# Last input block of an expert's up-projection as two full-height products, with every engine's order written anew

## The chip, the cores and the metric

The program runs on one core of a Trainium2 chip. A core has five engines that run at the same time, each on its own list of instructions, and that wait for each other through semaphores: TensorE (PE; its weight loads are shown apart as PEld), VectorE (DVE), ScalarE (ACT), GpSimd (POOL) and SyncE (SP), which here issues most of the DMA transfers. Products are accumulated in eight banks of PSUM, each 128 partitions by 512 float32 columns. The metric is the device time of one execution in microseconds (us); lower is better.

## The reference

An mLSTM-like recurrence is followed by two gated experts, all in float32:

```python
for t in range(S):                                   # S = 768, B = 2, H = 8, D = 40
    m_new = np.maximum(f_gate[:, :, t] + m, i_gate[:, :, t])
    ...
    C = f_stab[:, :, None, None] * C + i_stab[:, :, None, None] * np.einsum('bhd,bhe->bhde', vt, kt)
    n = f_stab[:, :, None] * n + i_stab[:, :, None] * kt
    h_tilde = np.einsum('bhde,bhe->bhd', C, qt)
    denom = np.maximum(np.abs(np.einsum('bhd,bhd->bh', n, qt)[:, :, None]), 1.0)
    y[:, :, t] = sigmoid(o_gate[:, :, t]) * h_tilde / denom
...
x = y.transpose(0, 2, 1, 3).reshape(1536, 320)
xn = x / rms(x) * rms_g                              # first expert
x = (silu(xn @ w_gate) * (xn @ w_val)) @ w_out       # 320 -> 1536 -> 320
x = (sigmoid(x @ w_gate2) * (x @ w_val2)) @ w_out2   # second expert, same sizes
```

## The kernel before

**The recurrence** is done in blocks of 128 steps: 6 blocks for each of 2 batches, so 12 units u of 128 tokens. For a unit, TensorE makes the decay exponents (`A`, line 425 for the first block of a batch, lines 432 and 435 later, from rows `rows3` that are sent there by DMA), the scores q·k (`S`, line 459, 40 rows high), the outputs (`O`, lines 483 and 492) and the update of the state (`C`, lines 519 and 521). The gates' running sums and maxima (`g1` to `g9`) are made once at the start on VectorE from the loaded gates `fi`; the running maximum goes to DRAM and back (`gO`, `gI`, tile `mD`) to be laid out for the later blocks, and then as `rows3` to the units from u = 2 on.

**The experts.** Each has 12 blocks m of 128 hidden columns, and tokens go in 3 groups g of 512, so there are 2 x 3 x 12 = 72 up-projections. To keep float32 accuracy with the fast fp32r format, each operand is split into a rounded part (hi) and the rest (lo), and three products are summed: hi·hi, lo·hi and hi·lo. The 320 input channels are two blocks of 128 and a last one of 64. In `xT` the last block stands twice, in partitions 0 to 63 and 64 to 127 (column blocks 2 for hi and 5 for lo). In the weights of that block, hi stands in one half of the partitions and lo in the other (`w_lo` writes the lo half). So one full product of x block 2 gives hi·hi and lo·hi together; only hi·lo is left over, from x block 5 and the hi half of the weights.

`up` (lines 622 to 634) makes the gate (`ug`, j = 0) and the value (`uv`, j = 1) of one block, each into one bank with the tag `wk`, of which there are four. In each, seven full products come from line 631: six for the first two blocks, and one for block 2. With the gate, line 634 makes the two leftover products of half height, the gate's from one half of the partitions and the value's from the other. Then ScalarE takes tanh (`ht`, line 638), VectorE multiplies (`hg`, `hv`), ScalarE rounds (`hh`), VectorE takes the rest (`hl`), and four `dn` of three products each (lines 662 to 664) add the block to the 320 outputs. `fn` and `st` take the outputs away.

**Weights** come as float64 in 48 halves of 544 KB (`wl`, SP queue), and ScalarE and VectorE turn each into hi and lo (`wp`, `wq`, `wb`, `wh`, `ws`).

**The order.** `ORDER` is a list of some 1,590 step names. The program is written by walking this list, so it fixes the order of each engine's instructions, those of the SP queue too. An engine takes its list in order, and what stands behind a waiting instruction waits too; only TensorE's weight loads (PEld) run beside the product ahead of them. Steps named `k` are products of zeros (line 391) into a bank that isn't used yet; they compute nothing and keep TensorE at work.

Of the kernel before, what the change touches and what calls it, by code (L numbers as in the profile page):

```python
# [44 lines left out]
HALF = (slice(0, 64), slice(64, 128))  # L45
# [11 lines left out]
Nd2 wq1 C2 Sb3 wp5 Sa3 Ab5 Ma3 Ws3 Lb3 Eg3 Lc3 U2 Ab4 Mb3 Xb4 Ga3 Gb3 P3 wh2 Oa3 Ob3 Ne2 wl0 k18 Nf2 wq5 ws2 wb5 Na3
Nb3 Lb4 Ld4 Xb5 k6 Wv3 cw4 La4 Nc3 Sa4 cw1 Sb4 Wp4 Ws4 Nd3 Dc3 C3 Ga4 Eg4 P4 wb1 wh1 U3 wl4 Mb4 Gb4 Lc4 wh5 wq4 wp4
Aa5 Oa4 Ob4 La5 Ld5 Ne3 ws1 Sb5 Na4 Nf3 ws5 wq0 Nb4 Ng2 Nc4 Aa6 Lb5 Dc4 Sa5 Wp5 Ws5 Wv4 C4 Xa5 Ma5 Lc5 P5 k45 Ga5 Ng3
Oa5 Nd4 Ne4 U4 d0.2 Xa6 Mb5 Gb5 wp0 wl9 wl10 Ob5 Na5 Wv5 Ma6 wb0 wh0 Nb5 Wp6 Eg5 Nc5 La6 Sa6 Ga6 Dc5 Aa7 Ab6 Xb6 Sb6  # L60
Ld6 C5 Ws6 wb4 Mb6 Nf4 P6 Lb6 Oa6 Gb6 Ob6 Nd5 Ab7 Ld7 La7 Lc6 U5 Ne5 Nf5 wh4 Xa7 Ma7 Na6 Ng4 ws4 Xb7 Eg6 Lb7 Lc7 Wp7
Ab9 Xb9 Mb7 Wv6 Nb6 Nc6 Nd6 Sa7 Sb7 C6 wl6 d0.4 wq6 Ws7 Gb7 Wv7 d0.1 P7 Aa8 Ga7 Oa7 Ne6 Dc6 wp6 Ob7 U6 wp9 La8 wq10
Ng5 ws0 Wp8 Ld8 Eg7 Na7 Nb7 Nc7 Ws8 Xa8 Sa8 Ab8 Xb8 Ma8 Ga8 Mb8 Sb8 Gb8 La9 C7 Lb8 Dc7 U7 Nd7 Wv8 P8 Eg8 Aa9 Xa9 d0.0
Mb9 Oa8 Lc8 Ld9 Ob8 Na8 Ma9 Sb9 Wp9 Nb8 Nc8 Ws9 Sa9 Ga9 t0.0 wb6 Gb9 Lb9 Eg9 Lc9 C8 P9 d0.3 Oa9 Ob9 Aa11 Dc8 Nf6 wl12
U8 Ng6 t0.1 x0.0 wh6 y0.0 wp10 Na9 Nb9 Nc9 x0.1 y0.1 Xa11 Ab10 Dc9 Xb10 t0.2 Wv9 C9 U9 Ld10 Ab11 La10 Wp10 Ws10 x0.2
Aa10 Xb11 Sa10 y0.2 Xa10 Wp11 Ma10 Ga10 Ma11 P10 t0.3 x0.3 y0.3 Mb10 Ne7 Nf7 Sb10 Gb10 wq9 La11 Sa11 ug0.0.0 Ld11 Ws11
Nd8 Ga11 Ng7 ht0.0.0 wb9 wb10 ws6 wh10 wh9 wp12 wq12 ug0.0.2 wl15 uv0.0.0 ht0.0.2 wq15 ws9 uv0.0.2 hg0.0.0 wb12
hv0.0.0 Nd9 hh0.0.0 ws10 wp15 hl0.0.0 hg0.0.2 hv0.0.2 wh12 Lb10 ws12 wl8 ug0.0.1 P11 wp8 ht0.0.1 hg0.0.1 hh0.0.2
hl0.0.2 wb15 Eg10 wl7 uv0.0.1 hv0.0.1 wq7 Oa10 Ob10 wh15 ws15 d0.5 Lb11 Eg11 Sb11 Ne8 wl16 Na10 wp7 wb7 Mb11 ug0.0.3
Gb11 wp16 hh0.0.1 wq8 ht0.0.3 wb8 wh8 dn0.0.0.0 Oa11 Ne9 Nf9 hg0.0.3 ws8 Nf8 d0.7 wq16 wb16 wl11 wp11 Ob11 wh7 ws7  # L70
Nb10 wh16 ug0.0.4 wq11 wl18 wp18 Nc10 uv0.0.4 Na11 Nb11 Ng8 t0.4 dn0.0.0.2 uv0.0.3 hl0.0.1 ht0.0.4 wl13 wq13 Nc11
# [75 lines left out]
def attention_then_two_moe(tc, fi, fir, qk, qt3, nat, w1, w2, rms_g, consts, out, order):  # L147
    nc = tc.nc
    ctx = ExitStack()
    cp = ctx.enter_context(tc.tile_pool(name="cp", bufs=1))  # L150
# [448 lines left out]
    for u in range(NU):  # L599
# [9 lines left out]
        for hh in range(2):  # L609
            h = "ab"[hh]  # L610
# [11 lines left out]
    def up(moe, g, m, j):  # L622
# [7 lines left out]
        for i, (a, b) in enumerate(terms):  # L630
            nc.tensor.matmul(o, lhsT=a, rhs=b, start=(j == 0 and i == 0), stop=(j == 1 and i == 6))  # L631
# [144 lines left out]
```

## Time and profile before

| | before |
|---|---|
| median of three runs | 532.69 us (530.91 to 535.45) |
| the profiled execution, device time | 533.24 us |
| its span, first to last instruction | 531.5 us |
| TensorE busy | 519.5 us (98%) |
| VectorE, ScalarE, GpSimd busy | 265.2, 213.4, 50.8 us |
| mean granted TensorE clock | 0.965 of full |

The span is 1.7 us less than the device time of the same execution. In the profile a line such as `L631 PE MATMUL wk<-xT,wH` is one group of instructions: the line of the kernel, the engine, the operation, and the tile written from the tiles read. The duration of one product is its passage through the array and overlaps the next one, so a product's cost is read from the distance between starts. A float32 product of the recurrence shows as two records.

### The profile page before, as it was taken

Reading aid. Unit: us, or ns where it says so; the run is one execution under the profiler, and the core shown is the slowest. Engines: PE = TensorE matmul, PEld = TensorE weight load, DVE = VectorE, ACT = ScalarE, POOL = GpSimd, SP = SyncE. Lnnn points to the kernel's source line nnn. Section 1 sums busy time; section 2 is a strip of 40 time slices with the busy share of each in tenths; the row PEclk is TensorE's granted clock in tenths of the full one; section 3 lists DMA queues with packets and bytes.
Section 4 is the critical chain, followed back from the end, with each engine's and each line's share of the span. In section 5 each row is a group of like instructions: output and inputs, shape, how many; then the busy total and the mean of one; then the engine's idle time right before and its main releaser. Section 6 shows DMA issues by size and latency. Waiting matters only on the chain.

```text
span 531.5 us, 7232 instructions
## 1 busy us (share of the span) xinstructions
PE 519.5 (98%) x2801; PEld 424.2 (80%) x2801; DVE 265.2 (50%) x504; ACT 213.4 (40%) x415; POOL 50.8 (10%) x102
## 2 busy tenths in 40 slices
PE   5999999999999999999999999999999999999997
PEld 4788989877887787878887778787887787887876
DVE  3546876497976344434455576745432222232213
ACT  3525553376675222223234568635431222222112
POOL 4024644200100000000000000000000000000000
PEclk9958997698999999999999999999999999999999
DMA  6475855264443010001002345502000000020001
GB/s 169 123 208 158 239 192 183 72 208 143 159 129 93 36 42 1 0 1 42 1 0 86 102 132 187 169 8 77 1 1 25 1 0 1 1 74 1 0 1 50
DMA packets 15252, 41.43 MB, mean 78 GB/s; under 512 B 1874, under 2 KB 6530, under 8 KB 15218
## 3 DMA queue, kind: packets, MB, share of 16 engines
q1 hardware_dynamic: 14882, 40.56, 25.0%
q8 instruction: 22, 0.36, 0.3%
q10 hardware_dynamic: 336, 0.41, 0.2%
q14 instruction: 12, 0.10, 0.1%
HBM read 38.77 MB, written 2.01 MB: 77 GB/s over the span
## 4 chain that ended last, share of the span: by engine, by line
PE 85%; ACT 0%; issue 0%
PE wk L631 46%; PE wk L634 6%; PE dn L662 5%; PE at L662 5%; PE dn L664 4%; PE at L664 4%; PE dn L663 4%; PE at L663 4%; PE at L492 2%; PE wk L583 2%; PE wk L459 2%; PE at L483 1%; PE at L519 1%; PE wk L432 0%; PE wk L435 0%; PE at L470 0%
## 5 line engine op out<-in xcount | busy, mean ns | idle before, releaser
L631 PE MATMUL wk<-xT,wH 128*128 128x512 f32 x720 | 216.8, 402 | 0.0
L631 PEld LDWEIGHTS wk<-xT,wH 128*128 128x128 f32 x720 | 128.5, 188 | 29.0 <-issue 8.1
L642 DVE SCALAR_TENSOR_TENSOR th<-th,wk 128x512 f32<-128x512 f32 x72 | 48.9, 685 | 112.8 <-PE wk L631 71.5
L631 PE MATMUL wk<-xT,wL 128*128 128x512 f32 x288 | 90.8, 397 | 0.0
L638 ACT ACTIVATE th<-wk 128x512 f32<-128x512 f32 x72 | 42.6, 596 | 114.1 <-PE wk L634 109.9
L650 ACT CAST hT<-th 128x512 fp32r<-128x512 f32 x72 | 44.1, 619 | 81.3 <-DVE th L642 29.9
L654 DVE TENSOR_TENSOR hT<-th,hT 128x512 fp32r<-128x512 f32 x72 | 48.9, 689 | 50.2 <-ACT hT L650 49.6
L631 PEld LDWEIGHTS wk<-xT,wL 128*128 128x128 f32 x288 | 54.5, 189 | 12.7
L662 PE MATMUL dn<-wH,hT 128*128 128x320 f32 x144 | 47.5, 330 | 0.0
L662 PE MATMUL at<-wH,hT 128*128 128x320 f32 x144 | 46.6, 324 | 0.0
L664 PE MATMUL dn<-wH,hT 128*128 128x320 f32 x144 | 44.6, 310 | 0.0
L664 PE MATMUL at<-wH,hT 128*128 128x320 f32 x144 | 44.5, 309 | 0.0
L663 PE MATMUL dn<-wL,hT 128*128 128x320 f32 x144 | 44.5, 309 | 0.0
L663 PE MATMUL at<-wL,hT 128*128 128x320 f32 x144 | 44.5, 309 | 0.0
L199 DVE SCALAR_TENSOR_TENSOR wT<-wT,w 128x544 int32<-128x544 int32 x48 | 34.3, 722 | 11.8 <-ACT wT L190 9.6
L190 ACT ACTIVATE wT<-wraw 128x544 f32<-128x544 f32 x48 | 33.0, 695 | 8.5 <-DVE wL L217 3.2
L634 PE MATMUL wk<-xT,wH 64*128 64x512 f32 x144 | 36.4, 500 | 0.0
L634 PEld LDWEIGHTS wk<-xT,wH 64*128 64x128 f32 x144 | 13.5, 184 | 26.9 <-issue 26.9
L206 ACT CAST wH<-wT 128x544 fp32r<-128x544 f32 x48 | 30.2, 641 | 11.0 <-DVE wT L199 8.9
L195 ACT ACTIVATE w<-wraw 128x544 int32<-128x544 uint16 x48 | 33.3, 698 | 1.2 <-DMA wraw<-in_w_dram 1.2
L459 PE MATMUL wk<-qk 40*128 40x128 f32 x192 | 29.4, 316 | 4.4 <-DMA qk<-in_qk_dram 4.4
L662 PEld LDWEIGHTS dn<-wH,hT 128*128 128x128 f32 x144 | 27.2, 189 | 6.6 <-issue 5.3
(114 smaller groups left out, 604.3 us busy)
## 6 DMA issues: line engine op xcount, KB each, us to landing
wraw<-in_w_dram SPq DMA_DIRECT2D x48, 544.0 KB
nat<-in_nat_dram SPq DMA_DIRECT2D x12, 324.0 KB
qk<-in_qk_dram SPq DMA_DIRECT2D x24, 160.0 KB
qt<-in_qt_dram SPq DMA_DIRECT2D x10, 180.0 KB
nat<-in_nat_dram SPq DMA_DIRECT2D x10, 180.0 KB
out_dram<-x2n SPq DMA_DIRECT2D x10, 160.0 KB
out_dram<-x2n ACTq DMA_DIRECT2D x2, 160.0 KB
rows<-x2n SPq DMA_DIRECT2D x6, 30.0 KB
```

Source lines behind the costliest of these rows:

```text
L195: nc.scalar.activation(t, upper, AF.Copy, scale=2.0 ** -13, bias=FLOOR)
L199: nc.vector.scalar_tensor_tensor(out=t, in0=t, scalar=3, in1=w3.pop(k), op0=ALU.logical_shift_left, op1=ALU.bitwise_or)
L459: nc.tensor.matmul(o[:, h * L:(h + 1) * L], lhsT=d["qk"][r, 1, h, :], rhs=d["qk"][r, 0, h, :], start=True, stop=True)
L631: nc.tensor.matmul(o, lhsT=a, rhs=b, start=(j == 0 and i == 0), stop=(j == 1 and i == 6))
L634: nc.tensor.matmul(act[moe, g, m][k], lhsT=hi[h, 128 * k:128 * (k + 1)], rhs=x[h, 5, :], start=(k == 1), stop=(k == 0))
L638: nc.scalar.activation(th, act[moe, g, m][0], AF.Tanh, scale=0.5)
L642: nc.vector.scalar_tensor_tensor(out=th, in0=th, scalar=1.0, in1=act[moe, g, m][moe], op0=ALU.add, op1=ALU.mult)
L650: Copy(hT[:, 0, :], act[moe, g, m, "h"])
L654: TT(out=hT[:, 1, :], in0=th, in1=hT[:, 0, :].bitcast(F32), op=ALU.subtract)
L662: nc.tensor.matmul(o, lhsT=hi, rhs=wo[0], start=(m == 0), stop=False)
L663: nc.tensor.matmul(o, lhsT=hi, rhs=wo[1], start=False, stop=False)
L664: nc.tensor.matmul(o, lhsT=lo, rhs=wo[0], start=False, stop=(m == NM - 1))
```

## The change

In `up`, the leftover product hi·lo of the last block is no longer made from a half-height weight for gate and value side by side. Instead x block 5 (lo, which stands in both halves of the partitions) is multiplied at full height with the same weights as x block 2, hi in one half and lo in the other. Gate and value each have eight full products in place of seven and a share in a pair of half-height ones; the small term lo·lo is now added too. Each bank's sum is opened and closed by its own eight products.

The list `ORDER` is new as a whole; two of its lines stand in the diff below. The steps in it are the same but for the `k` steps, which were 14 and are 11.

```diff
 ORDER = """
-cj cr cm cb ck wl3 gF gS La0 Lb0 g1 Ma0 g3 wp3 wq3 cs ci Sa0 gR Aa0 g2 ga gb ge Xa0 Sb0 wl2 gC Mb0 Ab0 Ga0 Xb0 Gb0 Ld2
+cj ci gS gF k46 ck k40 wl0 k28 gR k21 wl3 k31 cb k56 gC cm k55 cr g1 La0 k20 cs k33 Mb0 Ma0 Ma1 g3 Ab0 wq0 g2 gO k35
...
         terms = [((hi, lo)[r][:, at[r] + 128 * i:at[r] + 128 * (i + 1)], x[:, sl, :]) for r, i, sl in UP_TERMS]
-        terms.append((hi[:, 128 * j:128 * (j + 1)], x[:, 2, :]))
+        terms += [(hi[:, 128 * j:128 * (j + 1)], x[:, sl, :]) for sl in (2, 5)]
         for i, (a, b) in enumerate(terms):
-            nc.tensor.matmul(o, lhsT=a, rhs=b, start=(j == 0 and i == 0), stop=(j == 1 and i == 6))
-        if j == 0:
-            for k, h in enumerate(HALF):
-                nc.tensor.matmul(act[moe, g, m][k], lhsT=hi[h, 128 * k:128 * (k + 1)], rhs=x[h, 5, :], start=(k == 1), stop=(k == 0))
+            nc.tensor.matmul(o, lhsT=a, rhs=b, start=(i == 0), stop=(i == 7))
```

On TensorE, at the gate's up-projection of one block in the experts (`wH` and `wL` are one block's weights, `hT` the hidden values that `dn` takes), before:

```order
L631 MATMUL wk<-xT,wH_1526 128x512 x4
L631 MATMUL wk<-xT,wL_1527 128x512 x2
L631 MATMUL wk<-xT,wH_1526 128x512
L634 MATMUL wk<-xT,wH_1526 128x512 x2
L662 MATMUL at<-wH_1195,hT 128x320
```

and in the changed kernel:

```order
L658 MATMUL at<-wH_1180,hT 128x320
L659 MATMUL at<-wL_1181,hT 128x320
L660 MATMUL at<-wH_1180,hT 128x320
L630 MATMUL wk<-xT,wH_1715 128x512 x4
L630 MATMUL wk<-xT,wL_1716 128x512 x2
L630 MATMUL wk<-xT,wH_1715 128x512 x2
L582 MATMUL wk<-ident,x2n 128x128 x3
L630 MATMUL wk<-xT,wH_1715 128x512 x4
L630 MATMUL wk<-xT,wL_1716 128x512 x2
```

The two half-height rows of line 634 are gone, and the last `wH` row of each side counts two instead of one.

On TensorE at the very start of the program, from its first instruction, before (`masks` are constant tiles, `qk` the loaded queries and keys):

```order
L420 LDWEIGHTS masks
L420 MATMUL wk<-masks 128x512
L459 MATMUL wk<-qk 128x128 x4
L425 MATMUL wk<-x2n,ident 128x128 x4
L287 MATMUL at<-ident,x2n 128x16
L459 MATMUL wk<-qk 128x128 x4
L420 LDWEIGHTS masks
```

and in the changed kernel from the eighth of the zero products on (line 390, tile `junk`); seven like it stand ahead of these:

```order
L390 LDWEIGHTS junk
L390 MATMUL dn<-junk 128x512
L390 LDWEIGHTS junk
L390 MATMUL dn<-junk 128x512
L419 LDWEIGHTS masks
L419 MATMUL wk<-masks 128x512
L419 LDWEIGHTS masks
L419 MATMUL wk<-masks 128x512
L419 LDWEIGHTS masks
L419 MATMUL wk<-masks 128x512
L424 MATMUL wk<-x2n,ident 128x128 x4
L390 LDWEIGHTS junk
```

Nine zero products and three of the mask products now stand ahead of everything else, and the scores, which came second, come after them.

On TensorE ahead of the first product that reads `rows3`, before:

```order
L391 MATMUL dn<-junk 128x512
L391 LDWEIGHTS junk
L391 MATMUL dn<-junk 128x512
L459 MATMUL wk<-qk 128x128 x8
L432 LDWEIGHTS rows_0_75
L432 MATMUL wk<-pick,rows_0_75 128x512
```

and in the changed kernel:

```order
L518 MATMUL at<-wv,nat 120x123 x2
L518 MATMUL at<-wv,nat 120x82
L491 MATMUL at<-nat,E 128x41 x8
L518 MATMUL at<-wv,nat 120x123 x2
L518 MATMUL at<-wv,nat 120x82
L431 LDWEIGHTS rows_0_75
L431 MATMUL wk<-pick,rows_0_75 128x512
```

The second unit's outputs (line 492, now 491) and state update (line 519, now 518), which came later, now stand ahead of that product, and the zero products there are gone.

On the SP queue at the start (`wraw` is a half of the weights, `x2n<-in_fi` the gates of the first block), before:

```order
L186 DMA wraw<-in_w_dram 128x1088
L298 DMA x2n<-in_fi_dram 16x2x128
L407 DMA qk<-in_qk_dram 40x1024 x2
L410 DMA nat<-in_nat_dram 128x648
L300 DMA x2n<-in_fir_dram 80x256
L186 DMA wraw<-in_w_dram 128x1088
L302 DMA cst<-in_consts_dram 80x144
L415 DMA qt<-in_qt_dram 120x384
L306 DMA mD<-x2n 16x641
```

and in the changed kernel:

```order
L297 DMA x2n<-in_fi_dram 16x2x128
L185 DMA wraw<-in_w_dram 128x1088
L299 DMA x2n<-in_fir_dram 80x256
L185 DMA wraw<-in_w_dram 128x1088
L301 DMA cst<-in_consts_dram 80x144
L406 DMA qk<-in_qk_dram 40x1024 x2
L305 DMA mD<-x2n 16x641
L409 DMA nat<-in_nat_dram 128x648 x2
L276 DMA x2n<-mD 80x1x129
```

The gates' load has moved ahead of the first weight half, and the queries and keys behind the second. On POOL the fill of the zero tile and of `reset` (step `cr`), which `g1` reads, has moved from the front to behind the identity, the block pattern and the masks.

## Rows read from the trace of the kernel before

**Rows 1.** The page's first part: busy us (share of span) and instructions of each engine.

```profile
PE 519.5 (98%) x2801; PEld 424.2 (80%) x2801; DVE 265.2 (50%) x504; ACT 213.4 (40%) x415; POOL 50.8 (10%) x102
```

**Rows 2.** Stretches: width, then busy us of PE, PEld, DVE, ACT, POOL; clock, DMA, GB/s.

```profile
0.00:17.50 17.50, 10.99 (x43) 9.26 (x44) 5.41 (x15) 5.14 (x12) 5.46 (x24) 1.00 0.68 189
...
27.80:44.80 17.00, 17.00 (x82) 14.94 (x82) 8.21 (x20) 4.03 (x11) 4.02 (x7) 0.50 0.59 185
44.80:82.40 37.60, 37.23 (x332) 33.43 (x329) 29.50 (x68) 21.08 (x50) 21.62 (x31) 1.00 0.70 210
82.40:85.80 3.40, 3.40 (x18) 3.12 (x18) 2.27 (x4) 0.54 (x3) 2.84 (x5) 0.50 0.06 19
...
89.20:102.90 13.70, 13.70 (x70) 12.58 (x71) 7.62 (x16) 4.06 (x9) 1.59 (x2) 0.50 0.39 133
...
123.40:126.80 3.40, 3.40 (x10) 2.03 (x9) 1.24 (x3) 1.29 (x3) 1.23 (x3) 0.51 0.77 206
126.80:527.80 401.00, 401.00 (x2035) 322.21 (x2033) 185.34 (x326) 155.18 (x281) 7.12 (x19) 1.00 0.16 49
```

**Rows 3.** Groups by line: busy us, mean ns | idle before, what ended it.

```profile
L634 PE MATMUL wk<-xT,wH 64*128 64x512 f32 x144 | 36.4, 500 | 0.0
...
L634 PEld LDWEIGHTS wk<-xT,wH 64*128 64x128 f32 x144 | 13.5, 184 | 26.9 <-issue 26.9
...
L631 PEld LDWEIGHTS wk<-xT,wH 128*128 128x128 f32 x720 | 128.5, 188 | 29.0 <-issue 8.1 <-DVE xT L597 0.5
```

**Rows 4.** Timeline of PE in the steady stage: start, time, instruction.

```profile
399.80 1.09 PE L631 MATMUL wk<-xT,wH 128*128 128x512 f32 x4
...
403.05 0.31 PE L662 MATMUL dn<-wH,hT 128*128 128x320 f32 x1
...
403.94 1.08 PE L631 MATMUL wk<-xT,wH 128*128 128x512 f32 x4
...
405.32 0.40 PE L631 MATMUL wk<-xT,wH 128*128 128x512 f32 x1
405.66 0.50 PE L634 MATMUL wk<-xT,wH 64*128 64x512 f32 x2
406.09 1.20 PE L631 MATMUL wk<-xT,wH 128*128 128x512 f32 x4
407.13 0.62 PE L631 MATMUL wk<-xT,wL 128*128 128x512 f32 x2
...
407.82 0.31 PE L662 MATMUL dn<-wH,hT 128*128 128x320 f32 x1
```

**Rows 5.** Timeline of PE in the first 31 us.

```profile
7.12 2.07 PE L459 MATMUL wk<-qk 40*128 40x128 f32 x8 [4.09 <-DMA qk<-in_qk_dram]
...
22.73 1.71 PE L459 MATMUL wk<-qk 40*128 40x128 f32 x16
25.23 0.38 PE L432 MATMUL wk<-pick,rows 120*128 120x512 bf16 x1 [0.79 <-DMA rows<-x2n]
...
26.10 0.38 PE L391 MATMUL dn<-junk 128*128 128x512 bf16 x1
26.32 0.33 PE L470 MATMUL at<-rows,wide 120*120 120x128 bf16 x3
27.32 3.20 PE L492 MATMUL at<-nat,E 128*128 128x41 f32 x16 [0.66 <-DVE qt L475]
```

**Rows 6.** Timeline of DVE at the start.

```profile
0.89 0.11 DVE L377 MEMSET junk<- 128x64 uint32 x1 [0.89 <-PEq L766]
...
6.42 0.59 DVE L268 TENSOR_TENSOR_SCAN x2n<-x2n 16x128 f32<-16x128 f32 x1 [5.42 <-DMA x2n<-in_fi_dram]
```

**Rows 7.** Timeline of the SP queue: the round trip of the running maxima.

```profile
9.74 0.31 SPq L306 DMA_DIRECT2D mD<-x2n  x1
11.72 0.60 SPq L277 DMA_DIRECT2D x2n<-mD  x1
```

**Rows 8.** Stretch from 100 to 150 us, columns as in rows 2.

```profile
100.00:150.00 50.00, 50.00 (x276) 40.30 (x275) 39.28 (x81) 32.87 (x64) 7.03 (x13) 0.94 0.46 147
```

More of the change, by code (lines that the diff above doesn't have):

```diff
@@ L57 @@
[L57 to L71, printed above, removed]
@@ new lines @@
+uv0.1.1 ht0.1.1 hg0.1.1 dn0.1.0.2 hv0.1.1 dn0.1.0.0 uv0.1.3 hh0.1.1 hl0.1.1 t0.8 dn0.1.0.1 x0.8 dn0.1.0.3 y0.8
+dn0.1.1.3 hv0.1.3 dn0.1.1.0 dn0.1.2.0 hh0.1.3 dn0.1.1.1 wp26 hl0.1.3 dn0.1.2.3 dn0.1.2.1 ug0.1.4 uv0.1.4 ht0.1.4
+hg0.1.4 ug0.1.5 t0.9 dn0.1.3.3 x0.9 dn0.1.3.0 ht0.1.5 dn0.1.3.1 hg0.1.5 uv0.1.5 hv0.1.4 ug0.1.6 hv0.1.5 y0.9 dn0.1.1.2
+dn0.1.2.2 t0.10 hh0.1.4 uv0.1.6 x0.10 hl0.1.4 wq26 y0.10 hh0.1.5 ht0.1.6 dn0.1.4.1 hl0.1.5 ug0.1.7 wp24 hg0.1.6 wb26
+hv0.1.6 uv0.1.7 ht0.1.7 hg0.1.7 dn0.1.5.1 hv0.1.7 dn0.1.3.2 dn0.1.4.2 hh0.1.6 dn0.1.4.3 hl0.1.6 dn0.1.5.3 ug0.1.8
@@ new lines @@
+ug0.2.1 hv0.2.0 dn0.1.11.3 ht0.2.1 dn0.1.11.0 fn0.1.3 hg0.2.1 ug0.2.2 wq32 y1.0 hh0.2.0 fn0.1.0 hl0.2.0 t1.1
+dn0.1.11.2 x1.1 uv0.2.1 ht0.2.2 fn0.1.2 dn0.2.0.1 hv0.2.1 ug0.2.4 y1.1 hh0.2.1 hg0.2.2 hl0.2.1 dn0.1.11.1 ht0.2.4
+uv0.2.2 fn0.1.1 d1.5 d1.4 d1.7 d1.3 d1.6 dn0.2.0.2 hv0.2.2 t1.2 ug0.2.3 x1.2 hh0.2.2 hl0.2.2 dn0.2.0.0 ht0.2.3
+dn0.2.1.0 hg0.2.3 dn0.2.0.3 dn0.2.1.3 hg0.2.4 dn0.2.1.1 y1.2 dn0.2.2.1 uv0.2.3 dn0.2.1.2 hv0.2.3 dn0.2.2.2 wh26
+ug0.2.5 hh0.2.3 wh24 uv0.2.4 uv0.2.5 hv0.2.4 hl0.2.3 hh0.2.4 hl0.2.4 dn0.2.2.3 dn0.2.3.1 ht0.2.5 dn0.2.2.0 hg0.2.5
@@ new lines @@
+dn1.1.2.0 hl1.1.3 uv1.1.5 dn1.1.1.2 dn1.1.1.3 dn1.1.2.3 hh1.1.4 dn1.1.2.2 hl1.1.4 dn1.1.3.2 dn1.1.2.1 ht1.1.5
+dn1.1.3.1 dn1.1.4.2 hg1.1.5 uv1.1.6 hh1.1.5 ht1.1.6 hl1.1.5 dn1.1.4.1 dn1.1.3.3 dn1.1.5.1 dn1.1.3.0 dn1.1.4.0 t1.9
+ug1.1.7 x1.9 y1.9 hg1.1.6 dn1.1.5.2 ht1.1.7 ug1.1.8 hh1.1.6 uv1.1.7 dn1.1.4.3 hg1.1.7 dn1.1.5.3 hl1.1.6 t1.10 hh1.1.7
+ug1.1.9 ht1.1.8 hl1.1.7 x1.10 uv1.1.8 ht1.1.9 dn1.1.5.0 hg1.1.8 dn1.1.6.1 y1.10 dn1.1.7.1 hh1.1.8 dn1.1.6.0 hl1.1.8
+dn1.1.7.0 dn1.1.6.3 dn1.1.7.3 t1.11 dn1.1.8.0 x1.11 ug1.1.10 y1.11 uv1.1.9 ht1.1.10 uv1.1.10 hg1.1.9 dn1.1.6.2
@@ new lines @@
+hg1.1.10 dn1.1.7.2 hh1.1.9 dn1.1.8.3 hl1.1.9 ug1.1.11 uv1.1.11 ht1.1.11 hh1.1.10 dn1.1.9.0 hg1.1.11 ug1.2.0 dn1.1.8.1
+dn1.1.9.1 dn1.1.9.3 dn1.1.8.2 dn1.1.9.2 hh1.1.11 uv1.2.0 hl1.1.11 hl1.1.10 ht1.2.0 dn1.1.10.0 dn1.1.10.2 hg1.2.0
+ug1.2.1 hh1.2.0 ug1.2.2 ht1.2.1 dn1.1.11.0 dn1.1.11.2 dn1.1.10.1 dn1.1.10.3 dn1.1.11.3 uv1.2.1 fn1.1.3 dn1.1.11.1
+hg1.2.1 ug1.2.3 fn1.1.1 fn1.1.0 hh1.2.1 hl1.2.0 hl1.2.1 ht1.2.2 uv1.2.2 fn1.1.2 ht1.2.3 st1.2 st0.3 st0.0 st1.3
+dn1.2.0.1 hg1.2.2 st1.1 dn1.2.0.3 st0.2 dn1.2.0.2 hh1.2.2 st0.1 dn1.2.0.0 st1.0 hl1.2.2 dn1.2.1.0 dn1.2.1.2 uv1.2.3
@@ new lines @@
+dn1.2.2.0 hg1.2.3 ug1.2.4 ug1.2.5 uv1.2.5 ht1.2.5 hh1.2.3 hl1.2.3 dn1.2.3.0 ht1.2.4 uv1.2.4 dn1.2.2.2 hg1.2.4
+dn1.2.3.2 hg1.2.5 dn1.2.1.3 dn1.2.2.3 dn1.2.1.1 dn1.2.2.1 hh1.2.4 ug1.2.6 hh1.2.5 hl1.2.4 hl1.2.5 ug1.2.7 uv1.2.7
+ht1.2.7 ht1.2.6 dn1.2.4.2 hg1.2.7 dn1.2.3.1 dn1.2.5.2 uv1.2.6 dn1.2.3.3 hg1.2.6 ug1.2.8 hh1.2.6 hl1.2.6 dn1.2.4.0
+dn1.2.5.0 dn1.2.4.3 uv1.2.8 dn1.2.4.1 dn1.2.5.1 hh1.2.7 dn1.2.5.3 hl1.2.7 dn1.2.6.3 dn1.2.6.0 ht1.2.8 ug1.2.10 hg1.2.8
+hh1.2.8 uv1.2.10 hl1.2.8 ht1.2.10 dn1.2.6.2 hg1.2.10 dn1.2.7.2 dn1.2.7.0 dn1.2.8.0 dn1.2.6.1 ug1.2.11 dn1.2.7.1
@@ L144 @@
+ht1.2.11 dn1.2.7.3 hh1.2.10 dn1.2.8.2 ug1.2.9 hl1.2.10 uv1.2.9 ht1.2.9 uv1.2.11 hg1.2.9 hh1.2.9 hl1.2.9 dn1.2.8.1
+hg1.2.11 dn1.2.8.3 dn1.2.9.3 hh1.2.11 dn1.2.9.0 hl1.2.11 dn1.2.10.3 dn1.2.9.2 dn1.2.10.2 dn1.2.11.2 dn1.2.11.3 fn1.2.2
+dn1.2.10.0 fn1.2.3 st2.2 dn1.2.11.0 st2.3 dn1.2.9.1 fn1.2.0 dn1.2.10.1 st2.0 dn1.2.11.1 fn1.2.1 st2.1
 """
```

138 lines of the change are left out of this document (62 added, 76 removed).

## The prediction

> **What bounds the kernel now.** I read the page's busy shares first: TensorE is busy 98% of the span, VectorE half of it [rows 1]. Then the stretches, cut where the granted clock changes [rows 2]. From 126.8 to 527.8 us, three quarters of the span, TensorE is busy 401.00 of 401.00 us at full clock. Nothing that another engine does can shorten that stretch; only what TensorE spends on its own list can. Before 126.8 us the case is another: the clock stands at half (1.2 in place of 2.4 GHz) for 17.0, 3.4, 13.7 and 3.4 us, 37.5 us in all, in which it does 18.8 us of full-speed work, so 18.8 us are lost. The first stretch is slow too, though its row says 1.00: eight records of the scores at 7.12 took 2.07 us, and at 22.73 sixteen took 1.71 [rows 5]. That is about half speed from 7.1 to 17.5 us, 10.4 us of work at the price of 5.2 more. Ahead of it TensorE waits 4.09 us for the queries and keys.
>
> **The pair of half-height products.** What it costs is not its own duration but what it adds between its neighbours. From 399.80 to 403.05 there are 14 full products and nothing else: 3.25 us, 0.232 each. From 403.94 to 407.82 there are 14 full ones and one pair: 3.88 us [rows 4]. So a pair costs 3.88 - 3.25 = 0.63 us. The same rows say where: the product ahead of the pair holds TensorE 0.34 us (405.32 to 405.66) in place of 0.23, the pair 0.43, and the four products behind it 1.04 (406.09 to 407.13) in place of 0.93. The weight loader agrees: it stands idle before the 72 pairs for 26.9 us with nothing to wait for, some 0.37 us each, and 8.1 us before full loads in the same way [rows 3]; in the rest of the stage loads run under the product ahead of them. After the change two full products stand there: 2 x 0.232 = 0.464 us. Saved: 0.63 - 0.464 = 0.167 us in each of 72 blocks, **12.0 us**, all of it on the path, since TensorE is the path. Bounds: if the 0.11 behind the pair comes from something that remains, 0.34 - 0.23 + 0.43 - 0.464 = 0.076, so 5.5 us; the upper end is 12.0. I take 12.0, as both sums of 14 products lie in the same stage.
>
> The trace shows the two halves side by side, two products in one record of 0.50 us [rows 4]. The Trainium skill (TensorE: Matmul & The Clock Gate, Part 3: Packing small matmuls) speaks against this change there: products in different row groups run at once, so that the pair would cost about one product, 0.232 us, and the change would add 72 x 0.232 = 16.7 us. The trace has the halves overlap but not at that price; the skill's TensorEngine Tiling (Array Packing), Key Properties, says that a change of the tiling mode drains TensorE, and the gaps on both sides of the pair look like that.
>
> Two things that I cost at nothing: tanh no longer waits for line 634 but for the eighth product of the gate, at the same place of the list. The two banks are opened and closed as before in time, so the four `wk` banks turn over no slower. If TensorE is faster by 0.167 us in a block, VectorE and ScalarE must be too while weights are prepared; in the densest part VectorE is busy 39.28 of 50 us [rows 8], and 5% more is 41.2, so there is room.
>
> **The zero products.** One takes 0.22 us at full clock (26.10 to 26.32) [rows 5]. All 14 of before stand among work, behind 17 us. Of the 11 of now nine stand ahead of everything, where TensorE waited until 7.12: with three mask products, at half clock, 12 x 0.44 = 5.3 us, from about 1.0 us, when VectorE has zeroed the tile [rows 6], so they end at 6.3 and cost nothing. Two remain on the path. Saved: 12 x 0.22 = **2.6 us**.
>
> **The start.** The gates' scan waits 5.42 us for a load, until 6.42 [rows 6], because the load is issued behind 544 KB of weights. A small transfer through a less full queue, that of the maxima, took 11.72 - 9.74 = 2.0 us [rows 7]; first in the queue the gates should be there at some 3.5 us. The running sums then wait for POOL, whose fill of the zero tile is now late, and could start about 3 us sooner, and with them the maxima, the round trip through DRAM, and the rows that TensorE waits for at 25.23. Against this the queries and keys are now behind two weight halves and smaller loads, some 1.3 MB: at the 189 GB/s of the first stretch [rows 2] 7 us, so they land at 8 to 8.5 in place of 7.1, and between 6.3 and 8 TensorE has only four float32 products and two transposes of its own to do. Whether its clock is up by then I can't tell; if it is, up to 5.2 us more come back. Ends: 0 (the scores' delay eats the gain) and 3.3 + 5.2 = 8.5. I take **3**, near the gates' share alone.
>
> **The clock afterwards.** The first low stretch begins at 27.8, just after TensorE waited 0.79 us for the rows and 0.66 for `qt` [rows 5]. The outputs and state update of the second unit now stand ahead of the rows' first reader, so there is work to do during that wait. The other low stretches begin with TensorE busy all along (37.23 of 37.60 us ahead of the second) [rows 2], among scores that use 40 rows of the array and outputs 41 columns wide; the new order has the same products. Against it, eight zero products that stood behind the rows' first reader are gone from there. I take half of the first stretch's loss, 17.0 / 2 / 2 = **4 us**. Ends: all 18.8 comes back, or 20 us more at half clock, 10 lost.
>
> **The sum** is made against the profiled execution's 533.24 us, 0.55 above the median, less than the runs differ: 533.24 - 12.0 - 2.6 - 3 - 4 = 511.6, **512 us**. The last stores stay: in both orders one block of `dn`, `fn` and a store end the program.
>
> **The rivals.**
> 1. Only the pairs count: start and clock come out as before. 533.2 - 12.0 - 2.6 is 518.6; with the lower bound of the pair 525. For it: only the first low stretch began with a wait, and the scores' load comes later. 518 to 525, chance 0.20.
> 2. The clock stays up from the start on: the four low stretches and the slow first one go. 512 less the other 15 of 18.8 is 497; with one short drop 500 or so. For it: zero products now lift TensorE before any real work. Against: its falls after 44 us came without waits. 496 to 505, chance 0.13.
> 3. The pair takes only one product's place, as its two halves run side by side [rows 4], and the gaps around it have another cause that stays. Two products for one add 72 x (0.464 - 0.232) = 16.7 us: 533.2 + 16.7 - 9.6 = 540. Against: the two sums of 14. Chance 0.03.
> 4. The new order lets TensorE wait in the steady stage, say 0.2 us in each block for `hl` or a bank: 72 x 0.2 = 14.4 us, 526, and with no gain at the start 533. Against: 401.00 of 401.00 busy before, with other engines at half load. Chance 0.05.
> 5. Slower: without zero products among the attention the clock stays low. The stretch from 44.8 to 82.4 ran 37.6 us at full clock; at half it costs 37.6 more, so 516 + 37.6 = 553. It decides from 2 x (12.0 + 2.6 + 3) = 35 us of low clock more than the 37.5 of before. For it: the stretch was kept high with few wide products in it. Chance 0.04.
>
> **How the numbers follow.** My forecast, 505 to 518, has 0.55. The runs shown differ by 0.8%, so about 1%, 5.3 us, is what can be told from no change. Faster by more than 1% are the forecast, rivals 1 and 2 and some of 4: 0.92; within 1%: the rest of 4 and the edge of 1: 0.03; slower: 0.05. For 8 times in 10 the range leaves out the lower half of rival 2, rivals 3 and 5 and the slow end of 4: 502 to 524.
>
> **What would show it.** In the profile of the changed kernel, no line of half-height products; 16 full products of a block in 3.7 us; no idle of the weight loader for "issue" of that size. TensorE's busy time after the first `ug` shorter by about 12 us. The gates' scan on VectorE at 3 to 4.5 us; the first product that reads the rows at 21 to 23 us in place of 25.2; low clock of 25 to 35 us in all. I am wrong if two full products cost more than 0.47 us where the pair stood, if TensorE shows waits after 130 us, or if the low clock lasts well beyond 45 us.

## The result, and the profile after

Four runs of the changed kernel took 504.51 to 507.12 us, median 505.19, beside four of before at 530.91 to 551.28, median 534.07: a ratio of 0.9484 [0.9423, 0.9545]. Ratios, here and below, are taken between the faster executions of each kernel alone, so they are not those of the medians. The median is 6.8 us below the 512 that I predicted, and inside the range. Over all runs told of below, one and the same program took different times (before: 519.9 to 551.3 us), by the clock that it was granted in the part ahead of its steady stage, so I compare kernels by a second number as well, the span times its mean granted clock, which I call the **full-speed time**. It moves little between the runs of a kernel (before: a mean of 512.9 to 513.6 in each of four sets of runs, single ones from 511.1 to 516.0). By it the change is worth 513.2 - 491.6 = 21.6 us (513.2 is the mean of the four). A stretch at half pace that the profile still lists with a clock of 1.00, as the first one, counts in it as full-speed time.

The page's first part for the changed kernel, columns as in [rows 1]:

```profile
PE 496.5 (99%) x2798; PEld 432.8 (86%) x2798; DVE 262.3 (52%) x504; ACT 212.7 (42%) x415; POOL 47.4 (9%) x102
```

TensorE's busy time fell by 23.0 us and its idle time from 531.5 - 519.5 = 12.0 to 504.0 - 496.5 = 7.5. It is still the bound. Stretches of the changed kernel, cut where the granted clock changes, columns as in [rows 2]:

```profile
4.80:18.40 13.60, 10.83 (x82) 8.96 (x81) 8.91 (x24) 9.63 (x30) 1.19 (x3) 1.00 0.81 254
18.40:28.70 10.30, 10.30 (x52) 9.05 (x51) 5.12 (x12) 0.98 (x3) 3.38 (x9) 0.50 0.40 121
...
32.10:45.70 13.60, 13.60 (x72) 12.62 (x71) 5.84 (x14) 4.36 (x10) 6.05 (x12) 0.50 0.51 148
45.70:91.50 45.80, 45.80 (x424) 42.03 (x424) 37.97 (x87) 24.50 (x61) 22.96 (x38) 1.00 0.72 218
...
130.00:500.00 370.00, 370.00 (x1925) 322.60 (x1924) 167.95 (x289) 142.56 (x255) 3.16 (x14) 1.00 0.14 46
```

The clock is at half for 10.3 + 13.6 = 23.9 us in place of 37.5, and from 130 us on TensorE waits for nothing. The steady stage, in the timeline of TensorE, answers to [rows 4]:

```profile
398.46 1.09 PE L630 MATMUL wk<-xT,wH 128*128 128x512 f32 x4
399.40 0.63 PE L630 MATMUL wk<-xT,wL 128*128 128x512 f32 x2
399.86 0.62 PE L630 MATMUL wk<-xT,wH 128*128 128x512 f32 x2
400.32 0.31 PE L658 MATMUL dn<-wH,hT 128*128 128x320 f32 x1
```

Eight products take 400.32 - 398.46 = 1.86 us, 0.232 each, and the two last ones cost what the others do. The groups of the weight loader answer to [rows 3]:

```profile
L630 PEld LDWEIGHTS wk<-xT,wH 128*128 128x128 f32 x864 | 158.1, 188 | 30.2
L630 PEld LDWEIGHTS wk<-xT,wL 128*128 128x128 f32 x288 | 54.1, 188 | 12.7
```

The 26.9 us of idle ahead of half-height loads are gone, and the 8.1 that stood for "issue" at line 631 with them; the idle that is left names no releaser. The start, in TensorE's timeline, answers to [rows 5]:

```profile
1.06 3.93 PE L390 MATMUL dn<-junk 128*128 128x512 bf16 x9 [1.06 <-DVE x2n L266]
...
9.01 1.71 PE L458 MATMUL wk<-qk 40*128 40x128 f32 x16
...
16.82 1.13 PE L458 MATMUL wk<-qk 40*128 40x128 f32 x8 [2.18 <-DMA qk<-in_qk_dram]
...
25.95 0.63 PE L431 MATMUL wk<-pick,rows 120*128 120x512 bf16 x1
```

The first scores come later, at 9.01 in place of 7.12, but 16 of them take 1.71 us where 8 took 2.07: TensorE is at full pace from 4.8 us on, where before it was at half pace until 17.5. Then it waits 2.18 us for the second unit's queries and keys, until 16.82, and at 18.4 the clock falls; the waits of before for the rows and for `qt` [rows 5] are gone. The first product that reads the rows comes at 25.95, not earlier than the 25.23 of before, but with all of units 0 and 1 behind it, and the first up-projection starts at 91.6 us in place of 107.4. On VectorE the gates' scan came forward from 6.42 to 3.88, as said:

```profile
3.88 0.47 DVE L267 TENSOR_TENSOR_SCAN x2n<-x2n 16x128 f32<-16x128 f32 x1 [2.88 <-DMA x2n<-in_fi_dram]
```

### The profile page after: what moved, and what is told of

The parts are those of the page before. It is cut to its first block, busy times and chain, and to the rows that moved or that the text cites. A ratio compares the mean times of both kernels' runs of the same rounds, so it can differ in the third digit from the quotient of the medians.

```text
span 504.0 us, 7195 instructions
## 1 busy us (share of the span) xinstructions
PE 496.5 (99%) x2798; PEld 432.8 (86%) x2798; DVE 262.3 (52%) x504; ACT 212.7 (42%) x415; POOL 47.4 (9%) x102
## 4 chain that ended last, share of the span: by engine, by line
PE 96%; DMA 2%; DVE 1%; SPq 0%; ACT 0%; issue 0%; DVEq 0%; ACTq 0%
PE wk L630 53%; PE wk L458 5%; PE at L491 4%; PE at L658 4%; PE at L660 4%; PE at L659 4%; PE dn L658 4%; PE dn L660 4%; PE dn L659 4%; PE at L518 2%; PE wk L582 2%; PE at L482 2%; PE wk L431 1%; PE wk L434 1%; DMA qk<-in_qk_dram 1%; PE at L520 1%
## 5 line engine op out<-in xcount | busy, mean ns | idle before, releaser
L630 PE MATMUL wk<-xT,wH 128*128 128x512 f32 x864 | 240.9, 396 | 0.0
L630 PEld LDWEIGHTS wk<-xT,wH 128*128 128x128 f32 x864 | 158.1, 188 | 30.2
L658 PE MATMUL dn<-wH,hT 128*128 128x320 f32 x144 | 45.0, 312 | 0.0
L658 PE MATMUL at<-wH,hT 128*128 128x320 f32 x144 | 44.9, 312 | 0.0
L660 PE MATMUL dn<-wH,hT 128*128 128x320 f32 x144 | 44.5, 309 | 0.0
L660 PE MATMUL at<-wH,hT 128*128 128x320 f32 x144 | 44.4, 308 | 0.0
L642 DVE TENSOR_TENSOR th<-th,wk 128x512 f32<-128x512 f32 x36 | 24.5, 684 | 25.3 <-PE wk L630 24.6
L658 PEld LDWEIGHTS at<-wH,hT 128*128 128x128 f32 x144 | 27.1, 188 | 2.1 <-ACT x2n L665 0.3
L659 PEld LDWEIGHTS dn<-wL,hT 128*128 128x128 f32 x144 | 27.1, 188 | 1.9
```

What stands on the lines that cost most here:

```text
L630: nc.tensor.matmul(o, lhsT=a, rhs=b, start=(i == 0), stop=(i == 7))
L658: nc.tensor.matmul(o, lhsT=hi, rhs=wo[0], start=(m == 0), stop=False)
L659: nc.tensor.matmul(o, lhsT=hi, rhs=wo[1], start=False, stop=False)
L660: nc.tensor.matmul(o, lhsT=lo, rhs=wo[0], start=False, stop=(m == NM - 1))
```

## The experiments

Each was run beside the kernel before on the same chip. Times are medians, ratios are to before of the same set, and "full-speed" is the mean over a kernel's runs of span times mean granted clock.

| kernel | runs | us | lowest to highest | ratio | mean granted clock | full-speed |
|---|---|---|---|---|---|---|
| after | 4 | 505.19 | 504.51 to 507.12 | 0.9484 [0.9423, 0.9545] | 0.972 to 0.978 | 491.6 |
| e1_pairs_only | 4 | 516.34 | 510.67 to 540.35 | 0.9707 [0.944, 0.9975] | 0.930 to 0.986 | 501.9 |
| e2_order_only | 5 | 520.58 | 516.52 to 533.35 | 0.9821 [0.9549, 1.0093] | 0.952 to 0.987 | 506.9 |
| e3_pair_twice | 4 | 540.66 | 538.93 to 549.90 | 1.0259 [1.0089, 1.043] | 0.965 to 0.987 | 530.2 |
| e4_before_nine_zero_first | 4 | 532.90 | 521.45 to 540.23 | none | 0.941 to 0.980 | 510.0 |
| e5_no_zero_first | 4 | 507.93 | 501.71 to 512.43 | 0.9617 [0.9543, 0.9691] | 0.962 to 0.985 | 492.0 |
| e6_queries_sooner | 4 | 506.98 | 498.14 to 519.61 | 0.9564 [0.9469, 0.9658] | 0.951 to 0.993 | 492.2 |
| e7_fill_the_wait | 4 | 506.45 | 501.32 to 515.64 | 0.9577 [0.953, 0.9623] | 0.955 to 0.986 | 492.1 |
| e8_after_again | 4 | 512.67 | 499.05 to 522.84 | none | 0.940 to 0.990 | 491.3 |
| e9_tall_scores | 6 | 498.38 | 496.25 to 500.82 | 0.9542 [0.95, 0.9584] | 0.986 to 0.997 | 492.5 |
| e10_before_gates_first | 10 | 533.25 | 521.80 to 552.00 | 0.9993 [0.9961, 1.0024] | 0.929 to 0.987 | 512.8 |
| e11_before_no_zero | 4 | 534.31 | 522.83 to 537.80 | none | 0.948 to 0.975 | 508.4 |
| e12_zero_padded_keys | 6 | 497.79 | 496.94 to 499.43 | 0.9523 [0.9464, 0.9582] | 0.993 | 492.8 |

Before took 532.10, 524.49, 524.80 and 530.68 in the sets of e1 to e4, e5 to e8, e9 to e11, and e12; by full-speed time 513.6, 513.1, 513.3 and 512.9.

### The two halves of the change, apart

e1 is before with the changed `up` and the old order:

```diff
-        terms.append((hi[:, 128 * j:128 * (j + 1)], x[:, 2, :]))
+        terms += [(hi[:, 128 * j:128 * (j + 1)], x[:, sl, :]) for sl in (2, 5)]
...
-            nc.tensor.matmul(o, lhsT=a, rhs=b, start=(j == 0 and i == 0), stop=(j == 1 and i == 6))
-        if j == 0:
...
+            nc.tensor.matmul(o, lhsT=a, rhs=b, start=(i == 0), stop=(i == 7))
```

> The changed up-projection (eight full products a side, no pair) in the order of before, its 14 zero products included. Theory: the pair cost 0.167 us more than two full products in each of 72 blocks, all on TensorE's path, so 12.0 us less than before: about 521 to 522. Rival, that most of the gain came with the new order (start and clock) and the pair gave little: 528 or more, 5.5 us less at best. Rival, that a pair takes one product's place: 72 x 0.232 = 16.7 us more than before, about 550.

e2 is the changed kernel with the same lines turned back.

> The new order with the up-projection of before (seven full products a side and the pair). Theory: the whole gain of some 28 us less the pairs' 12, so 16 us less than before, 517 to 518, with the first product of line 631 near 91.6 us as in the changed kernel. Rival, that the order only helps together with the full products: near 530.

By full-speed time the products alone give 513.6 - 501.9 = 11.7 us and the order alone 513.6 - 506.9 = 6.7. Together that is 18.4, and both at once give 22.0 against the same 513.6 (the changed kernel ran in another set). So in the new order the pairs cost more than in the old: 506.9 - 491.6 = 15.3. Part of it stands in the view of TensorE's waits of e2, from 95 to 525 us (engine, line, waited for; total us, times, longest):

```profile
PE wk L633 <- DVE th L641: 1.4, 1, 1.4
PE wk L630 <- DVE th L645: 0.3, 1, 0.3
```

The same view of the changed kernel, from 92 to 500 us, is empty. With the pair, `ug` already writes the value's bank, and so needs a second free bank one step sooner than with two full products; the new order is made for the latter. That explains 1.7 of the 15.3 - 11.7 = 3.6; the rest I have not shown. The medians, which take in the clock, point the same way with wide intervals, and no more can be read from them.

### What of the pair is running, and what is the change of height

e3 makes the pair twice, so that its bank sums hold the leftover term two times:

```diff
-            for k, h in enumerate(HALF):
-                nc.tensor.matmul(act[moe, g, m][k], lhsT=hi[h, 128 * k:128 * (k + 1)], rhs=x[h, 5, :], start=(k == 1), stop=(k == 0))
+            for n in range(2):
+                for k, h in enumerate(HALF):
+                    nc.tensor.matmul(act[moe, g, m][k], lhsT=hi[h, 128 * k:128 * (k + 1)], rhs=x[h, 5, :],
+                                     start=(k == 1 and n == 0), stop=(k == 0 and n == 1))
```

> Kernel before, with the half-height pair of each block issued twice in a row (its term counts double, so the output is another). It tells the pair's running cost from the cost of entering and leaving half height. Theory, that the gaps on both sides are paid once per change of height and the pair itself takes 0.43 us: 72 x 0.43 = 31 us more than before, about 563. Rival, that two halves side by side run at the price of one full product and all the rest is the change of height: 72 x 0.23 = 17 us more, about 550. Rival, that all of the 0.63 us belongs to each pair: 45 us more, about 578.

TensorE's timeline of e3 in the steady stage:

```profile
406.51 0.40 PE L631 MATMUL wk<-xT,wH 128*128 128x512 f32 x1
406.84 0.74 PE L635 MATMUL wk<-xT,wH 64*128 64x512 f32 x4
407.51 1.19 PE L631 MATMUL wk<-xT,wH 128*128 128x512 f32 x4
408.53 0.63 PE L631 MATMUL wk<-xT,wL 128*128 128x512 f32 x2
```

Two pairs hold TensorE from 406.84 to 407.51, 0.67 us, where one held it 0.43 [rows 4]: the second pair costs 0.24 us, about one full product. The whole kernel says the same: 530.2 - 513.6 = 16.6 us, 0.23 for each of 72 pairs. The time ahead (406.51 to 406.84, 0.33) and behind (407.51 to 408.53, 1.02 for four) is as with one pair. The groups of the weight loader show that only the first pair waits for its weights, since 288 half-height loads have no more idle before them than 144 had [rows 3]:

```profile
L635 PEld LDWEIGHTS wk<-xT,wH 64*128 64x128 f32 x288 | 21.5, 184 | 26.6 <-issue 26.6
```

So of the pair's 0.63 us some 0.23 is running and 0.40 is the passage to half height and back: 0.10 ahead, 0.11 behind, and 0.43 - 0.24 = 0.19 between. The weight loader's timeline of before, beside the products in [rows 4], says what these may be:

```profile
405.10 0.19 PEld L631 LDWEIGHTS wk<-xT,wH 128*128 128x128 f32 x1
405.65 0.19 PEld L634 LDWEIGHTS wk<-xT,wH 64*128 64x128 f32 x2 [0.37 <-issue]
406.09 0.76 PEld L631 LDWEIGHTS wk<-xT,wH 128*128 128x128 f32 x4 [0.24 <-issue]
```

The load of a full product starts 0.22 us ahead of it (405.10 and 405.32). The pair's load starts only with the pair (405.65 and 405.66), and the next full load only with its product (406.09). So one load on the way in (184 ns) and one on the way out (188 ns) run under no product ahead of them, 0.37 us together, nearly the whole 0.40; that these are the cost is argued from this view, not tested. My own expectation, 0.43 for the running, fell; the rival's held.

### The start

e4 puts nine of before's zero products at its very front; e5 takes the nine from the front of the changed kernel; e10 lets before load the gates ahead of the first weight half; e11 takes all 14 zero products out of before:

```diff
e4
-cj cr cm cb ck wl3 gF gS ...
+cj k46 k40 k28 k21 k56 k55 k20 k33 k35 cr cm cb ck wl3 gF gS ...
e5
-cj ci gS gF k46 ck k40 wl0 k28 gR k21 wl3 k31 cb k56 gC cm k55 cr g1 La0 k20 cs k33 Mb0 ...
+cj ci gS gF ck wl0 gR wl3 cb gC cm cr g1 La0 cs Mb0 ...
e10
-cj cr cm cb ck wl3 gF gS La0 ...
+cj cr cm cb ck gF wl3 gS La0 ...
```

> Kernel before with nine more zero products ahead of everything on TensorE, as in the new order. Theory, that TensorE ran at half clock from 7.1 to 17.5 us for want of work before 7.1: the scores at 7 us take about 0.9 us for eight records in place of 2.07, and the time falls by 0 to 5 us, as far as the rows at 25.2 us don't hold it back. Rival, that the clock at the start doesn't matter because the rows' chain sets the time of 25.2 us: within 1 us of before.

> The changed kernel without its nine zero products at the start (the mask products come first). Theory, that they lift TensorE's clock before the real work: granted clock rises near 10 us or later in place of 4.8, TensorE works at half pace until then, 2 to 5 us more than the changed kernel, 507 to 510; span times clock stays near the changed kernel's 491.6 within what lies hidden at the start. Rival, that the queries' and rows' transfers set the time of the start anyway: within 1 us of 505.

> Kernel before with the gates' load issued ahead of the first weight half in the SP queue, and nothing else. Theory, that this alone brings the rows 2 to 3 us sooner: first scan on VectorE near 3.9 in place of 6.4, first product that reads the rows near 22 to 24, span times clock 1 to 3 us under the 513 of before. Rival, that TensorE's slow first units set that time: the scan is sooner, the rows' product moves by less than 1 us, span times clock stays at 513.

> Kernel before without any of its 14 zero products. Theory, that each costs its 0.22 us on the path: span times clock 3 us under before, 510. Rival, that they hide in waits: 513 as before. What they do for the clock: if they hold it up, the granted clock is lower than in the kernel before (0.932 to 0.987 in 14 runs, mean 0.966), by chance alone no different.

In e10 the scan came forward as far as in the changed kernel, and the rows' first reader by 0.27 us, in the timelines of VectorE and TensorE (the first and the second row):

```profile
3.90 0.47 DVE L268 TENSOR_TENSOR_SCAN x2n<-x2n 16x128 f32<-16x128 f32 x1 [2.89 <-DMA x2n<-in_fi_dram]
...
24.96 0.38 PE L432 MATMUL wk<-pick,rows 120*128 120x512 bf16 x1
```

The full-speed time fell by 0.5 us, within what the sets of before differ by, and the ratio is 0.9993. Nothing waits for the gates that early: TensorE comes to the rows only when it is done with what stands ahead of them, at half pace. In e4's profiled execution the zero products ran from 1.06 us, yet the scores behind them took the old 2.07 us for eight, after a wait of 1.22 us for the queries; the pace rose at 17.2 us, near the 17.5 of before:

```profile
1.06 4.02 PE L391 MATMUL dn<-junk 128*128 128x512 bf16 x9 [1.06 <-DVE x2n L267]
...
6.73 2.07 PE L459 MATMUL wk<-qk 40*128 40x128 f32 x8 [1.22 <-DMA qk<-in_qk_dram]
```

That execution stands at 511.3 us of full-speed time. Two of the other three of e4 stand at 506.7 and 509.3, below every run of before, so the nine may have brought the full pace forward there; no trace shows it.

In e5, without the nine, TensorE first works at 4.11 us and is at full pace at the scores, 10.26 us (the sixteen take 1.71 us again). So the gates do not make the start, and with the new order the nine zero products are not needed for it: taking them away costs 0.4 us (492.0 against 491.6). In the profiled executions the full pace comes at 4 to 10 us in each kernel of the new order (e7 and e9 lose it again at 10.7 and 11.8) and at 15 to 19 in each of the old one. e11 is worth 513.3 - 508.4 = 4.9 us of full-speed time, 0.35 for each product removed, but its mean granted clock in these runs was 0.948 to 0.975, and its median was no better than that of before.

### The clock behind the start

e6 exchanges the loads `Lb1` and `La1` in the changed kernel, so that the second unit's queries come sooner; e7 fills the wait for them with nine zero products; e8 is the changed kernel once more:

```diff
e6
-Lb0 ga Aa0 Lb1 gb ... Aa1 La1 gx ...
+Lb0 ga Aa0 La1 gb ... Aa1 Lb1 gx ...
e7
-Na0 Eg0 p0 Nb0 Sa1 ...
+Na0 Eg0 p0 Nb0 k0 k1 k2 k3 k4 k5 k6 k7 k8 Sa1 ...
```

> The changed kernel with two loads of the second unit exchanged in the SP queue: its queries and keys ahead of its 324 KB of values. In the changed kernel TensorE waits 2.18 us for them and the clock falls at 18.4, 1.6 us after the wait. Theory, that this wait is worth its own length and makes the clock fall: no wait at the second unit's scores, no low clock before 30 us, 2 to 7 us less, 498 to 503. Rival, that the clock falls from the 40-row scores and 41-column outputs anyway: only the wait goes, 2 us less or nothing, with a low stretch still starting between 17 and 22 us.

> The changed kernel with nine zero products put into the 2.18 us wait ahead of the second unit's scores (9 x 0.22 = 2.0 us). Theory, that the wait lets the clock fall at 18.4: the low stretch of 10.2 us there goes or comes later, up to 5 us less, about 500 to 503. Rival, that work of other kinds sets it: the low stretch stays, 505 to 507, as the fill then delays the scores at half clock.

> The changed kernel once more, beside the others on the same chip, to see how far its low clock wanders from run to run: span times granted clock 491 to 492 in every run whatever the time; the time 503 to 510 if its low clock holds near 24 us, up to 520 if it wanders as it does in the kernel before (523 to 540 us in seven runs).

Neither moved the full-speed time, and neither kept the clock up. e7 does not wait after 7.6 us, and still its clock was at half from 10.7 to 20.9 us, ahead of and under most of the fill, and again from 34.6 to 68.7 us, as its timeline of TensorE shows for the first of the two (sixteen products of line 492 take 1.88 us at full pace, nine zero products 2.0):

```profile
13.55 3.48 PE L492 MATMUL at<-nat,E 128*128 128x41 f32 x16
...
18.95 3.09 PE L391 MATMUL dn<-junk 128*128 128x512 bf16 x9
```

In e6 the wait for the queries went, but one of 2.55 us for ScalarE's `E` came in its place, and the clock fell within it. e6 took 498.14 us in its profiled execution with a clock of 0.993, and 503.20 to 519.61 in the others. The same program once more, e8, gave from 499.05 to 522.84 us. Stretches of e8, columns as in [rows 2]:

```profile
18.20:48.90 30.70, 30.70 (x150) 26.89 (x149) 12.69 (x30) 7.75 (x19) 10.85 (x21) 0.50 0.38 119
...
59.20:66.00 6.80, 6.80 (x35) 6.10 (x33) 3.50 (x8) 2.23 (x5) 1.69 (x3) 0.50 0.12 40
```

37.5 us at half clock, against 23.9 in the first execution of the same program, and TensorE busy in all of them. So how long the clock is low is no property of this change: a run's loss, its span times one less its mean clock, was 16.0 us on average over 42 runs of before (5.2 to 37.3) and 15.5 over the 8 of the changed kernel (5.0 to 31.3).

e9 asks which products go with it. The scores are 40 rows high; here they are taken over all 104 rows of the tile, in which the other half's heads are summed in (so the output is another):

```diff
-            for r in (0, 64):
-                nc.sync.dma_start(out=d["qk"][r:r + D], in_=qk[u, r:r + D])
+            nc.sync.dma_start(out=d["qk"], in_=qk[u])
...
-        r = slice(64 * hh, 64 * hh + D)
+        r = slice(0, QR)
```

> The changed kernel with its scores made over 104 rows of the array in place of 40: queries and keys of both halves come in one load with the zero rows between them, and each product sums both (the scores are of other heads too, so the output is another). Same products, same columns, same count. Theory, that the clock falls because the scores, a quarter of the recurrence's products, use 40 rows of 128: the granted clock stays at or above 0.99 in nearly all runs, 495 to 500. Rival, that waits and the short 41-column outputs set it: clocks from 0.94 to 0.99 as in the changed kernel, 499 to 523. Span times clock 491 to 493 in both.

e12 makes the same with the reference's output: the keys of each half lie in a tile of 104 rows whose other rows are zero.

```diff
+    kz = [ap.tile([QR, 2, 4, L], F32, name=f"kz{i}", bufs=1) for i in range(2)]
...
+            d["q"] = ap.tile([QR, 4, L], F32, tag="q", name="q")
+            nc.sync.dma_start(out=d["q"], in_=qk[u, :, 0])
+            for hh, r in enumerate((0, 64)):
+                nc.sync.dma_start(out=kz[u % 2][r:r + D, hh], in_=qk[u, r:r + D, 1])
...
-            nc.tensor.matmul(o[:, h * L:(h + 1) * L], lhsT=d["qk"][r, 1, h, :], rhs=d["qk"][r, 0, h, :], start=True, stop=True)
+            nc.tensor.matmul(o[:, h * L:(h + 1) * L], lhsT=kz[u % 2][:, hh, h, :], rhs=d["q"][:, h, :], start=True, stop=True)
```

> The changed kernel with scores 104 rows high that compute the right thing: the keys of the two halves lie in tiles whose other rows are zeroed once at the start, so each product sums one head and zeros. 53 KB more per unit are loaded, in three transfers in place of two, and VectorE zeroes two tiles of 104 x 1024 before the gates arrive. Theory, that the height of the scores in the array, not the values in it, keeps the clock up: granted clock 0.985 or more in nearly all runs, 495 to 501, against 499 to 523 of the changed kernel. Rival, that rows of zeros count for nothing: clocks from 0.94 to 0.99, 499 to 523. Span times clock 491 to 494 in both.

Both stayed at 0.986 or more in all six runs of each, where the kernels with scores of 40 rows, in the same sets or in others, went as low as 0.929; of 25 runs of the new order with 40 rows, 4 reached 0.986. The changed kernel itself was not run in these two sets. Both kernels also load the queries and keys in another number of transfers, e9 in one and e12 in three, which was not tried by itself. By full-speed time e12 gains nothing (492.8 against 491.6), since a score product's passage is as long as before (its median is 275 ns against 272), and there is a little more to wait for; what it gains is the clock. Its stretches:

```profile
31.60:38.40 6.80, 6.12 (x30) 6.15 (x31) 2.51 (x7) 2.34 (x5) 3.20 (x6) 0.50 0.65 198
38.40:84.06 45.66, 45.41 (x435) 43.59 (x435) 38.13 (x87) 23.99 (x60) 22.93 (x38) 1.00 0.75 230
```

One low stretch of 6.8 us is left. It begins within a wait of 2.33 us, and the one low stretch of e9's profiled execution, from 11.8 to 25.5 us, within one of 2.96, as that of e6 within one of 2.55. These are the waits in TensorE's timelines of e12, e9 and e6:

```profile
32.28 3.75 PE L461 MATMUL wk<-q,kz 104*128 104x128 f32 x16 [2.33 <-DMA kz<-in_qk_dram]
...
12.05 3.78 PE L457 MATMUL wk<-qk 104*128 104x128 f32 x16 [2.96 <-DMA qk<-in_qk_dram]
...
20.63 3.61 PE L491 MATMUL at<-nat,E 128*128 128x41 f32 x16 [2.55 <-ACT E L445]
```

So in the two traces with scores of 104 rows no fall is left with TensorE busy; the falls that are left come in a wait. In e12 the first up-projection starts at 84.06 us in place of 91.6. With a median of 497.79 us, 496.94 to 499.43, e12 beats both kernels: it is 1.5% below the first runs of the changed kernel and 2.9% below its second set, though those ran in other sets.

## Why the prediction was right, and where it was not

**The pairs: right in size, wrong inside.** 12.0 us were predicted and 11.7 measured with the old order. From the first up-projection to the last product before takes 420.4 us, 1.7 of them lost at low clock, and e1 407.4 for the same list of steps: 11.3 less. (The changed kernel takes 408.7 there, with 16 more TensorE instructions behind that point.) The distance between sums of 14 products was the right way to cost it, because it takes in what stands on both sides. What I then wrote of the inside, that the pair itself takes 0.43, was not: 0.23 is running, 0.40 is the change of height. Of the Trainium skill's two rules neither gives the result by itself. Products in different row groups run at once (TensorE: Matmul & The Clock Gate, Part 3: Packing small matmuls): e3 agrees, 0.24 us for an extra pair. A change of the tiling mode drains TensorE (TensorEngine Tiling (Array Packing), Key Properties): the other 0.40 fits that, though no run shows the drain itself. Rival 3 failed there: the gaps did not have another cause that stays; they left with the pair [rows 3, 4]. Of rival 4 there is no trace, as no wait stands behind 92 us; it does appear with the pairs left in the new order (e2), 1.7 us. That also shows that the two banks are not opened as before in time: the value's is now opened one step later, which I had put at nothing.

**The zero products and the start: too little, from terms that were wrong.** I predicted 2.6 + 3 = 5.6 us; the order alone gave 6.7, and on top of the pairs 501.9 - 491.6 = 10.3. It lies ahead of the first up-projection: that is reached after 107.4 us in before and 91.6 in the changed kernel, at full speed after 107.4 - 17.1 = 90.3 and 91.6 - 11.9 = 79.7. The step "near the gates' share alone" failed: that share is at most 0.5 (e10), and the rows' first reader came 0.7 us later, not 2 to 4 sooner. What I had only as the upper end came true instead, the full pace from the start, for 5.2 us [rows 5]. An account from the rows, argued and not tested part by part: the pairs 11.7, idle time 12.0 - 7.5 = 4.5, the half pace of the start 5.2, twelve zero products on the path 2.6, less the 3.9 that nine of them now take as busy time at the front, is 20.1 of 21.6. The 0.22 for a zero product was too low by what e11 shows, 0.35. Why the full pace comes early with the new order even without the zero products, and late in e4's trace with them, stays open: the order of the first masks, exponents and scores wasn't tried piece by piece. One rival, untested, is the height of the scores: in the old order scores of 40 rows are nearly the first products, in the new one full-height exponents stand ahead of them.

**The clock afterwards: a gain that came, but is not the change's.** I took 4 us; between the profiled executions it was 18.6 - 12.6 = 6 (span times one less the mean clock: 531.5 x 0.035 and 504.0 x 0.025). But the profiled execution of e8 lost 511.0 x 0.038 = 19.4 with the same program, and on average the two kernels lose the same, 16.0 and 15.5. The gain was luck. The step that failed is that work in place of the wait for the rows would bring back half of the first low stretch: that wait went, another of 2.18 us came 8 us sooner, and the clock fell 1.6 us behind it. Where that one is filled (e7) the clock fell too, at 10.7 us, with TensorE busy. Most of the 6.8 us by which the time came out below 512 is this: 533.24 - 505.69 = 27.5 us between the two profiled executions is about 21.5 of full-speed time and 6 of clock, where my terms had 17.6 and 4. The times of rival 2 (499.05) and of rival 1 (522.84) both occur in e8, so the clock does not tell these rivals from my forecast; rival 5 did not come.

What stays open is why scores of 104 rows keep the clock up where TensorE is busy, and whether e12 without its wait of 2.33 us would keep it up throughout.

## What to carry to other kernels

Cost a product of another height by the distance between its neighbours: most of its price is the entering and the leaving, which a full-height product with zeros or with a term that isn't needed doesn't pay. When the clock wanders between executions, compare the span times the mean granted clock first; here single values of before differed by 4.9 us and the means of its sets by 0.7, where single times differed by 31. And look at how many rows the products use in a stretch whose clock falls while TensorE is busy: padding with zeros cost 1.2 us of full-speed time here (492.8 against 491.6) and took the wandering away.

## What the runs showed of the hardware

- Going from full to half height and back costs 0.40 us each time, and pairs in a row pay it once (e3); in before the weight loads on the way in and out, 184 and 188 ns, start only with their products, where the load ahead of them starts 0.22 us before its product.
- The mean granted clock was 0.993 in six runs with scores padded with zeros to 104 rows, and 0.929 to 0.993 in the runs with 40 rows (e12, and the other kernels). The falls that are left with 104 rows begin in waits of 2.33 and 2.96 us (e12, e9).
- One program without any change took from 519.9 to 551.3 us, while span times mean granted clock stayed within 511.1 to 516.0; the low stretches lie in the first 127 us of before's trace and the first 66 of e8's, with TensorE busy in them.
